# Re-ordering a fused attention and gated-MLP kernel: weight loads on one queue, a re-ordered prologue, earlier key features, PV in other slots

## The chip, the cores and the metric

The kernel runs on one core of one Trainium2 chip. The metric is the device time of one execution in microseconds (us). Five engines do the work: TensorE (PE) multiplies matrices, VectorE (DVE), ScalarE (ACT) and GpSimd (POOL) work on elements, and SyncE (SP) mostly issues DMA transfers. Within the fast state, the mean clock granted to PE still takes a few values, mainly 0.998 to 1.0, 0.993 and 0.987; this will matter.

## The reference, cut to what matters

```python
def reference(A_x, A_wq, A_wk, A_wv, A_wo, A_beta, B_x, B_w_gate, B_w_up, B_w_down, c, w_mod):
    # x: 2048 x 448; 16 heads of 28; 4 segments of 512 rows; MLP width 1792
    mod = (silu(c) @ w_mod)                       # six rows: sa, ca, ga, sb, cb, gb
    h = layernorm(x) * (1 + ca) + sa
    x = x + ga * attention(h, wq, wk, wv, wo, beta)
    h = layernorm(x) * (1 + cb) + sb
    x = x + gb * ((sigmoid(h @ w_gate) * (h @ w_up)) @ w_down)
    return x
# attention, per segment: causal softmax inside the segment (p @ v), plus a read of a
# memory M of all earlier segments: phi(q) @ M / (phi(q) @ z); then M += phi(k)^T v.
# The two are mixed with g = sigmoid(beta). phi(t) = t + 1 for t > 0, else exp(t).
```

## The kernel before: the parts that matter

The program is one hand-made order of instructions. Each engine executes its own share in that order. A queue `fill` holds jobs (projections, memory updates, output projection `wo`, MLP halves), and the loop over segments and head groups puts them between the three groups of logits of a unit. `later` delays cheap instructions in the order so that they don't block an engine.

```python
def mem_k(s, hc):                 # key features of the memory; 'pk' is their transpose, by DMA on SP
    ...
    phi(kT_of[s][:, hc, :], 3500, ("pk", s),
        lambda e: nc.sync.dma_start_transpose(pk[:, hc, :, :], e[:]))

def norm_t(self, i):              # layer norm of segments 2 and 3: transpose by DMA on SP
    self.norm(i)
    ...
    nc.sync.dma_start_transpose(self.h[:, :, i * P:(i + 1) * P], self.xn[:, i, :])   # 'hT'

def bias_rows():                  # sa @ wq, sa @ wk, sa @ wv, all in one PSUM buffer
    bp = m_f32("bp")
    for k in range(NK):
        for i, w in enumerate((wq_st, wk_st, wv_sb)):
            nc.tensor.matmul(bp[HP * i:HP * i + 1, 0:D], lhsT=sa_bf[...], rhs=w[...], ...)
    ...

def load_eng(w_sb):               # the up weights 'wu' are issued by ACT, all else by SP
    return nc.scalar if w_sb is wu_sb else nc.sync

early_loads = [load_wo, lambda: load_x(nc.sync, 3 * TPS, 4 * TPS), load_wm5] \
    + [piece_wd(f, min(f + 4, NFC)) for f in range(0, NFC, 4)] \
    + [piece(wg_sb, B_w_gate, k) for k in range(NK)] + [piece(wu_sb, B_w_up, k) for k in range(NK)]
fill.extend(sp(load_bw2))
fill.extend(spread(j0[3:6] + sp(late_consts) + j0[6:] + ln1_pe_jobs(1) + [ln1_start(2)] + m[0][0:1]
                   + j1[:4] + [ln1_start(3)] + j1[4:8], early_loads[:11], 1))
fill.extend(j1[8:] + [(1800, prep_b1)])
fill.extend(spread(j2[:2] + m[0][1:] + j2[2:3] + m[1][0:1] + j2[3:8], early_loads[11:], 2))
...
for s in range(NSEG):
    for hc in range(NHC):
        prev = (s, hc - 1) if hc else (s - 1, NHC - 1)
        for g in range(3):
            logits(s, hc, g)
            if fill and fill[0][1] is gate_up2:       # the up half of a gate-up pair
                fill.popleft()[1](); ...
            if prev[0] > 0 and g == 0:
                mem_read(*prev)
            if prev[0] >= 0 and g == 1:
                pv(*prev)
            ...
            debt = run_fill(pace[0] + debt)
            if prev[0] >= 0 and g == 2:
                otr(*prev)                            # DMA transpose 'oT' of the attention output
last = NSEG - 1
dj = down_jobs(last - 1)
mem_read(last, NHC - 1)
run_fill(2000)
pv(last, NHC - 1)
...
```

The softmax here doesn't subtract the row's maximum and nothing guards it: scores larger than these inputs give would overflow.

## Time and profile before

| | before |
|---|---|
| time, median of 3 runs | 262.42 us (261.68 to 262.72) |
| time of the profiled run | 263.58 us, clock 0.993 |
| span of the trace | 261.9 us |

The page's first part gives each engine's busy time; the clock row (PEclk) gives the granted clock in tenths, in 40 slices of the span. The prediction below shows both and reads the waits from them. The profiled run was 1.2 us slower than the median.

Two views of the kernel before: the first is SP's order of time (start, duration, line, output and input, number of instructions). The columns are the same in all orders of time below.

```profile
33.23 3.61 SPq L376 DMA_TRANSPOSE pk<-e  x2
36.93 5.31 SPq L283 DMA_TRANSPOSE hT<-xn  x4
42.33 1.22 SPq L376 DMA_TRANSPOSE pk<-e  x1
43.60 1.26 SPq L486 DMA_TRANSPOSE oT<-ou  x1
44.95 1.22 SPq L376 DMA_TRANSPOSE pk<-e  x1
```

The four hT transposes of segment 2 are issued in 5.31 us. The last pk goes out at 44.95. The second view is PE's order of time behind them; a bracket holds the idle time before a row and what ended it.

```profile
42.62 0.29 PE L414 MATMUL lg<-qT,kT 28*128 28x256 bf16 x4
43.62 1.02 PE L339 MATMUL pq<-hT,wq_sb 128*128 128x512 bf16 x4 [0.71 <-DMA hT<-xn]
...
49.24 0.38 PE L387 MATMUL dM<-vt,pk 128*128 128x116 bf16 x4 [2.27 <-DMA pk<-e]
```

PE begins segment 2 at 43.62 us and the last quarter of the first memory update at 49.24 us.

### The profile page before, as it was taken

Reading aid. Unit: us, or ns where it says so; the run is one execution under the profiler, and the core shown is the slowest. Engines: PE = TensorE matmul, PEld = TensorE weight load, DVE = VectorE, ACT = ScalarE, POOL = GpSimd, SP = SyncE. Lnnn points to the kernel's source line nnn. Section 1 sums busy time; section 2 is a strip of 40 time slices with the busy share of each in tenths; the row PEclk is TensorE's granted clock in tenths of the full one; section 3 lists DMA queues with packets and bytes.
Section 4 is the critical chain, followed back from the end, with each engine's and each line's share of the span. In section 5 each row is a group of like instructions: output and inputs, shape, how many; then the busy total and the mean of one; then the engine's idle time right before and its main releaser. Section 6 shows DMA issues by size and latency. Waiting matters only on the chain.

```text
span 261.9 us, 5307 instructions
## 1 busy us (share of the span) xinstructions
PE 243.3 (93%) x2066; PEld 113.3 (43%) x2066; DVE 175.6 (67%) x410; ACT 140.5 (54%) x175; POOL 78.5 (30%) x146
## 2 busy tenths in 40 slices
PE   7799997688988899899999999999998999999994
PEld 2434443333543343454544343445343445433352
DVE  5779899382898668878966576895754676544411
ACT  1368887549868597874617758534572210133300
POOL 3399255221346213243522121453030014000000
PEclk9999999997999999999999999999999999999999
DMA  5999934899912302210231010104200003200011
GB/s 147 276 249 255 327 75 101 146 178 194 97 28 54 29 16 46 57 23 20 46 91 40 20 22 0 24 20 95 58 15 9 20 0 67 86 0 0 3 35 35
DMA packets 40992, 19.66 MB, mean 75 GB/s; under 512 B 29704, under 2 KB 40072, under 8 KB 40968
## 3 DMA queue, kind: packets, MB, share of 16 engines
q1 hardware_dynamic: 39032, 16.92, 30.4%
q10 hardware_dynamic: 1936, 2.41, 4.2%
q8 instruction: 16, 0.26, 0.4%
q14 instruction: 8, 0.07, 0.1%
HBM read 10.67 MB, written 1.84 MB: 48 GB/s over the span
## 4 chain that ended last, share of the span: by engine, by line
PE 70%; DVE 10%; DMA 9%; ACT 5%; issue 3%; POOL 1%; ACTq 0%; SPq 0%; DVEq 0%
PE dps L546 16%; PE gps L520 13%; PE ups L537 12%; PE pq L339 5%; PE gps L525 5%; PE pwo L495 5%; PE acc L439 5%; PE lg L414 4%; DMA hT<-xn 3%; ACT pT L417 3%; DMA wm<-in_w_mod_dram 2%; PE pv L351 2%; DMA wv_sb<-in_A_wv_dram 2%; DVE st L265 2%; DVE xn L273 2%
## 5 line engine op out<-in xcount | busy, mean ns | idle before, releaser
L417 ACT ACTIVATE pT<-lg 128x2048 bf16<-128x2048 f32 (+1 forms) x48 | 76.8, 1599 | 26.8 <-PE lg L414 26.8
L528 ACT ACTIVATE tt<-gps 128x512 f32<-128x512 f32 x56 | 30.4, 595 | 57.5 <-PE gps L525 57.5
L425 POOL TENSOR_SCALAR_AFFINE_SELECT pT<-pT 128x512 bf16<-128x512 bf16 x64 | 41.5, 664 | 63.9 <-ACT pT L417 63.9
L540 DVE SCALAR_TENSOR_TENSOR fT<-tt,ups 128x512 bf16<-128x512 f32 x56 | 36.9, 685 | 31.4 <-PE ups L537 29.2
L546 PE MATMUL dps<-wd_sb,fT 128*128 128x448 bf16 x224 | 43.9, 352 | 0.0
L520 PE MATMUL gps<-hT,wg_sb 128*128 128x512 bf16 x168 | 41.2, 379 | 1.0 <-DVE t L451 1.0
L537 PE MATMUL ups<-hT,wu_sb 128*128 128x512 bf16 x168 | 41.1, 381 | 0.0
L546 PEld LDWEIGHTS <-fT 128*128 128x128 bf16 x224 | 21.5, 98 | 19.9 <-issue 0.2
L269 POOL TENSOR_SCALAR rs<-mv 128x1 f32<-128x1 f32 (+2 forms) x21 | 5.9, 282 | 61.2 <-DVE mv L266 58.4
L520 PEld LDWEIGHTS <-wg_sb 128*128 128x128 bf16 x168 | 15.8, 98 | 19.1 <-DVE t L451 1.6
L537 PEld LDWEIGHTS <-wu_sb 128*128 128x128 bf16 x168 | 14.2, 97 | 20.7 <-issue 6.6
L265 DVE BATCH_NORM_STATS2 st<-x_sb 128x6 f32<-128x448 bf16 x32 | 19.8, 619 | 2.5 <-DMA x_sb<-in_A_x_dram 2.0
L414 PE MATMUL lg<-qT,kT 28*128 28x512 bf16 (+3 forms) x256 | 17.3, 302 | 4.0 <-ACT pT L417 3.9
L439 PE MATMUL acc<-vt,pT 128*128 128x29 bf16 x640 | 18.7, 175 | 1.5 <-DVE t L470 1.0
L439 PEld LDWEIGHTS <-pT 128*128 128x128 bf16 x640 | 17.6, 96 | 5.2 <-issue 2.6
L273 DVE TENSOR_SCALAR xn<-x_sb,mv,rs 128x448 bf16<-128x448 bf16 x32 | 15.9, 512 | 4.6 <-POOL rs L270 4.6
L339 PE MATMUL pq<-hT,wq_sb 128*128 128x512 bf16 x64 | 17.8, 395 | 0.7 <-DMA hT<-xn 0.7
L550 DVE TENSOR_TENSOR ot<-dps,x_sb 128x448 bf16<-128x448 f32 x16 | 9.9, 621 | 12.2 <-PE dps L546 9.5
L525 PE MATMUL ups<-hT,wgu_sb 64*128 64x512 bf16 x56 | 17.5, 382 | 0.5 <-DVE t L451 0.5
L339 PE MATMUL pq<-hT,wk_sb 128*128 128x512 bf16 x64 | 16.5, 379 | 1.3 <-DVE t L451 1.1
L525 PE MATMUL gps<-hT,wgu_sb 64*128 64x512 bf16 x56 | 16.9, 381 | 0.0
L414 PEld LDWEIGHTS <-kT 28*128 28x128 bf16 x256 | 5.6, 91 | 22.1 <-issue 21.1
(100 smaller groups left out, 271.5 us busy)
## 6 DMA issues: line engine op xcount, KB each, us to landing
wm<-in_w_mod_dram SPq DMA_DIRECT2D x5, 392.0 KB, 9.2
out_dram<-ot SPq DMA_DIRECT2D x16, 112.0 KB, 1.7
x_sb<-in_A_x_dram SPq DMA_DIRECT2D x3, 448.0 KB, 4.8
wd_sb<-in_B_w_down_dram SPq DMA_DIRECT2D x3, 448.0 KB, 9.9
wg_sb<-in_B_w_gate_dram SPq DMA_DIRECT2D x3, 448.0 KB, 9.1
wu_sb<-in_B_w_up_dram ACTq DMA_DIRECT2D x3, 448.0 KB, 5.9
wm<-in_w_mod_dram ACTq DMA_DIRECT2D x1, 392.0 KB
wo_sb<-in_A_wo_dram SPq DMA_DIRECT2D x4, 98.0 KB
```

The lines of the kernel that those rows point to most:

```text
L265: nc.vector.bn_stats(st[:], self.srcs[i])
L339: nc.tensor.matmul(pq[:, 0:L], lhsT=head_cols(w_sb, k, hc), rhs=h[:, k, :], start=(k == 0), stop=(k == NK - 1))
L414: nc.tensor.matmul(lg[:, hs, wid:wid + nq], lhsT=kT[r, hc, kb * P:(kb + 1) * P], rhs=qT[r, hc, kb * P:L], start=True, stop=True, tile_posi ...
L417: nc.scalar.activation(pT[:, :, w0:w0 + wid], lg[:, :, 0:wid], AF.Exp, scale=scale)
L425: nc.gpsimd.affine_select(out=blk, in_=blk, compare_op=ALU.is_ge, fill=0.0, base=0, pattern=[[0, 4], [1, P]], channel_multiplier=-1)
L439: nc.tensor.matmul(accv[:, qb, hs, 0:ME], lhsT=pT[:, hs, c0:c0 + P], rhs=vt[:, kb, hc * 4 + hs, 0:ME], start=(kb == 0), stop=(kb == qb))
L520: nc.tensor.matmul(g[:, 0:L], lhsT=wg_sb[:, k, f], rhs=h[:, k, :], start=(k == 0), stop=False)
L525: nc.tensor.matmul(dst[:, 0:L], lhsT=wgu_sb[r:r + LW, f], rhs=h[r:r + LW, 3, :], start=first, stop=not first, tile_position=(r, 0))
L528: nc.scalar.activation(tt[:], g[:, 0:L], AF.Tanh, scale=0.5)
L537: nc.tensor.matmul(u[:, 0:L], lhsT=wu_sb[:, k, f], rhs=h[:, k, :], start=False, stop=(k == 2))
L540: nc.vector.scalar_tensor_tensor(ft[:], tt[:], 1.0, u[:, 0:L], op0=ALU.add, op1=ALU.mult)
L546: nc.tensor.matmul(dp[:, 0:D], lhsT=fT_of[(s, fc)][:, t * P:(t + 1) * P], rhs=wd_sb[:, fc, :], start=(fc == 0), stop=(fc == NFC - 1))
```

## The change

The intent is to take the last DMA issues off ACT, where one of them blocked an eviction and an exp, and to put them on SP right behind the other weights; to let the first projections start before the value weights are there; to issue the first key features' transposes earlier; and to run PV in a place where PE waited. The diff, cut to its core:

```diff
-    NWARM, EARLY, KEEP = (20, 2), 2400.0, (0, 2, 2, 4)
+    NWARM, EARLY, KEEP = 18, 2400.0, (0, 2, 2, 4)
...
-    def bias_rows():
-        bp = m_f32("bp")
+    def bias_rows(ws):
+        bp = warm[:, 4 - len(ws), :]
...
-    mod_cols(((0, 0), (1, 1)), False)
-    warm_up(NWARM[1])
+    mod_cols(((0, 0),), warm[:, 1, :])
+    for t in range(TPS):
+        ln0.norm(t)
+    mod_evac(((0, 0),))
...  # transposes of segment 0, then the second modulation, then q's bias alone:
+    evac_q, = bias_rows((wq_st,))
...
+    j0[0][1]()                                   # first q projection
+    evac_k, evac_v = bias_rows((wk_st, wv_sb))   # the biases that need wv
...
-    def load_eng(w_sb):
-        return nc.scalar if w_sb is wu_sb else nc.sync
...
-    fill.extend(spread(j0[3:6] + sp(late_consts) + j0[6:] + ln1_pe_jobs(1) + [ln1_start(2)] + m[0][0:1]
-                       + j1[:4] + [ln1_start(3)] + j1[4:8], early_loads[:11], 1))
+    fill.extend(spread(j0[3:6] + sp(late_consts) + j0[6:11] + m[0][0:1] + j0[11:] + ln1_pe_jobs(1) + [ln1_start(2)]
+                       + j1[:4] + [ln1_start(3)] + j1[4:8], early_loads, 1))
-    fill.extend(spread(j2[:2] + m[0][1:] + j2[2:3] + m[1][0:1] + j2[3:8], early_loads[11:], 2))
+    fill.extend(j2[:2] + m[0][1:] + j2[2:3] + m[1][0:1] + j2[3:8])
...
-                if prev[0] >= 0 and g == 1:
+                if prev[0] >= 0 and (g == 1 or g == 0 and s > 1 and pace[0] + debt <= 0) and prev in todo:
+                    todo.remove(prev)
                     pv(*prev)
...
+    if fill and fill[0][1] is gate_up2:
+        fill.popleft()[1]()
     mem_read(last, NHC - 1)
```

So there are five parts: the **prologue**, the **loads** on SP, the earlier **key job** (`m[0][0:1]`), the **PV** slots, and the **tail** (the up half ahead of the last memory read).

More of the change, by code (lines that the diff above doesn't have):

```diff
@@ L210, with mod_cols @@
     cp_of = {}
-    def mod_cols(jobs, evac=True):
-        cp = cp_of[0] = m_f32("cp")
+    def mod_cols(jobs, cp=None):
+        evac = cp is None
+        cp = cp_of[0] = m_f32("cp") if evac else cp
         for j, vi in jobs:
@@ L624, in pad_copy, with evac @@
             eng.tensor_scalar(dst, src, by, None, op0=ALU.mult)
-    def bias_rows():
-        bp = m_f32("bp")
+    def bias_rows(ws):
+        bp = warm[:, 4 - len(ws), :]
         for k in range(NK):
             r = P if k < 3 else LW
-            for i, w in enumerate((wq_st, wk_st, wv_sb)):
+            for i, w in enumerate(ws):
                 nc.tensor.matmul(bp[HP * i:HP * i + 1, 0:D], lhsT=sa_bf[0:r, k:k + 1], rhs=w[0:r, k, :],
                                  start=(k == 0), stop=(k == NK - 1), tile_position=(0, HP * i))
-        heads = lambda i: bp[HP * i:HP * i + 1, 0:D].rearrange("p (h d) -> p h d", d=Dh)
-        return [lambda: nc.scalar.copy(wq_sb[LW:LW + 1, 3, :, 0:Dh], heads(0)),
-                lambda: nc.vector.tensor_copy(wk_sb[LW:LW + 1, 3, :, 0:Dh], heads(1)),
-                lambda: nc.scalar.copy(wv_sb[LW:LW + 1, 3, :], bp[2 * HP:2 * HP + 1, 0:D])]
-    warm_up(NWARM[0])
+        def evac(i):
+            return lambda copy, dst: copy(dst, bp[HP * i:HP * i + 1, 0:D].rearrange("p (h d) -> p h d", d=Dh))
+        return [evac(i) for i in range(len(ws))]
+    warm_up(NWARM)
     ln0 = LN([x_sb[:, t, :] for t in range(TPS)], ("1", 0))
@@ L644 @@
     silu_ops()
-    mod_cols(((0, 0), (1, 1)), False)
-    warm_up(NWARM[1])
+    mod_cols(((0, 0),), warm[:, 1, :])
+    for t in range(TPS):
+        ln0.norm(t)
+    mod_evac(((0, 0),))
     pts = [m_bf16("lntr") for _ in range(NK)]
     for t in range(TPS):
-        ln0.norm(t)
-        if t == 1:
-            mod_evac(((0, 0), (1, 1)))
         for kc in range(NK):
             nc.tensor.transpose(pts[kc][:, t * P:(t + 1) * P], ln0.xn[:, t, kc * P:(kc + 1) * P], ident[:])
-    for k in range(2):
-        pad_copy(nc.scalar, wq_sb, wq_st, k)
-        pad_copy(nc.vector, wq_sb, wq_st, 2 + k)
+    mod_cols(((1, 1),), warm[:, 2, :])
     for kc in range(NK):
         ln0.pe_evac(pts[kc], kc, True)
-    evac_q, evac_k, evac_v = bias_rows()
-    evac_q()
+    mod_evac(((1, 1),))
+    evac_q, = bias_rows((wq_st,))
+    for k in range(NK):
+        pad_copy(nc.vector, wq_sb, wq_st, k)
+    evac_q(nc.scalar.copy, wq_sb[LW:LW + 1, 3, :, 0:Dh])
     for k in range(NK):
         pad_copy(nc.vector, wk_sb, wk_st, k)
-    evac_k()
-    evac_v()
+    tick(0)
+    j0, j1, j2, j3 = [proj_jobs(s) for s in range(NSEG)]
+    j0[0][1]()
+    evac_k, evac_v = bias_rows((wk_st, wv_sb))
+    evac_k(nc.vector.tensor_copy, wk_sb[LW:LW + 1, 3, :, 0:Dh])
+    evac_v(nc.scalar.copy, wv_sb[LW:LW + 1, 3, :].rearrange("p (h d) -> p h d", d=Dh))
     for k in range(NK):
@@ L671 @@
     ln1_start(1, True)[1]()
-    tick(0)
-    j0, j1, j2, j3 = [proj_jobs(s) for s in range(NSEG)]
-    for c, fn in j0[:3]:
+    for c, fn in j0[1:3]:
         fn()
@@ L694, in piece @@
             r = slice(0, LW) if w_sb is wg_sb else slice(LW, P)
-            return lambda: load_eng(w_sb).dma_start(wgu_sb[r, :], w[3 * P:D, :])
-        return lambda: load_eng(w_sb).dma_start(w_sb[:, k, :], w[k * P:(k + 1) * P, :])
+            return lambda: nc.sync.dma_start(wgu_sb[r, :], w[3 * P:D, :])
+        return lambda: nc.sync.dma_start(w_sb[:, k, :], w[k * P:(k + 1) * P, :])
     def piece_wd(f0, f1):
@@ L725 @@
     debt = 0.0
+    todo = {(s, hc) for s in range(NSEG) for hc in range(NHC)}
     for s in range(NSEG):
```

## The prediction

> **What bounds the kernel now.** I read the page first, then the waits of TensorE (PE), then the PE order of time in 5 us stretches, then the chain of work that ended last around the worst gaps, and the SyncE (SP) and ScalarE (ACT) queues beside them.
>
> ```profile
> PE 243.3 (93%) x2066; PEld 113.3 (43%) x2066; DVE 175.6 (67%) x410; ACT 140.5 (54%) x175; POOL 78.5 (30%) x146
> PEclk9999999997999999999999999999999999999999
> ```
>
> PE is busy 243.3 of 261.9 us, so 18.6 us of gaps are the whole stock that a reordering can draw on; no matmul of any weight is removed. The clock row has one dip, in the tenth slice (58.9 to 65.5 us). The waits say which gaps they are (engine, line, what it waited for; total, times, longest):
>
> ```profile
> PE lg L414 <- ACT pT L417: 3.9, 5, 1.8
> PE dM L387 <- DMA pk<-e: 2.3, 1, 2.3
> ...
> PE cp L224 <- DMA wm<-in_w_mod_dram: 1.0, 1, 1.0
> PE pq L339 <- DMA hT<-xn: 0.7, 1, 0.7
> ...
> PE mem L463 <- ACT tt L528: 0.5, 1, 0.5
> PE acc L439 <- ACT tt L528: 0.5, 1, 0.5
> ```
>
> The 3.9 us are one wait of 1.82 us (60.09 us), two of 0.78 us (106.51 and 150.71 us) and two of 0.25 us. The longest is explained by the ACT order of time and by the chain:
>
> ```profile
> 55.88 0.63 ACT L361 ACTIVATE e<-kT 128x512 bf16<-128x512 bf16 x1
> 58.00 0.49 ACTq L695 DMA_DIRECT2D wgu_sb<-in_B_w_up_dram  x1
> 58.53 0.58 ACT L342 CAST qT<-pq 128x512 bf16<-128x512 f32 x1 [2.01 <-PE pv L351]
> 59.01 1.03 ACT L417 ACTIVATE pT<-lg 128x1024 bf16<-128x1024 f32 x1
> ```
> ```profile
> 51.34 6.64 DMA hT<-xn
> 57.98 0.02 issue
> 58.00 0.49 ACTq L695
> ```
>
> ACT finishes an exp at 56.5 us and then stands in front of a weight-load issue until 58.0: the instruction order shows that each DMA waits for the DMA eight before it, and this one's lane belonged to the last hT transpose, which landed at 57.98. The label "<-PE pv" is misleading. Behind the issue stand the qT eviction and the exp that frees the logits buffer; PE gets it at 60.09 us. Straight after that gap the clock is low:
>
> ```profile
> 60.42 2.55 PE L351 MATMUL pv<-wv_sb,hT 128*128 128x448 bf16 x8
> 62.76 1.90 PE L339 MATMUL pq<-hT,wq_sb 128*128 128x512 bf16 x4
> ```
>
> The same groups take 1.68 (at 81.49) and 1.03 us elsewhere: 0.87 + 0.87 = 1.74 us lost, with 0.66 of the clock granted in 60 to 65 us.
>
> **What the Trainium skill says.** (1) "DMA: Bandwidth & Descriptors", Issuing engines are not separate DMA queues: loads issued by different engines share the same 16 DMA engines; issuing from several saves only sequencer time. The trace agrees and shows the price: the ACT issue cost 0.49 us plus 1.5 us of blocking. (2) "TensorE: Matmul & The Clock Gate", What's actually happening: the gate follows activity in a free-running window of about 3.4 us. The trace agrees in kind (the dip lasts about 4 us and follows the gap), but 2.27 us of idle at 47 us caused no dip, so I can't call it certain. (3) The same page, Architectural detail: ACT and DVE are strict FIFO. The blocked qT eviction above agrees. (4) "Perfetto Trace Analysis", DMA Instruction — HWDGE: the profiled length of an issue is descriptor generation, not data movement. The trace: each DMA transpose holds SP 1.22 us, and two loads of wd held it 1.90 and 2.66 us.
>
> **The change part by part.**
>
> *Loads.* All four wu/wgu issues (1.6 MB: three of 448 KB and one of 224 KB) go from ACT, 49.2 to 58.5 us, to SP right behind the wg loads, which SP finished issuing at 26.2 us; SP then idles until 33.2. ACT loses four issues and their waits. The 1.82 us gap goes: without the issue, qT and exp run 56.5 to 58.05 us, and PE came free at 58.27. **-1.8**. If PE then has no gap there, the dip has no cause: -1.74, which I take at three in four: **-1.3**.
>
> *Earlier key features.* The first memory-feature job moves ahead of the last value projection and four transposes. In the order, SP's pk transposes become three before the four hT transposes of segment 2 and one after, instead of two, four, one, then oT, then one. Before, the last pk was issued at 44.95 us behind an oT that waited for its input, and took 4.2 us to land; PE waited for it 2.27 us until 49.24. Now it follows hT directly, at about 42 to 43 us, and lands by 46 (transposes land in 2.3 to 3.6 us). The wait goes: **-2.3**.
>
> *Prologue.* Before, the first logits run at 16.52 and their exp at 16.97. The chain is: wv landing (12.54), 12 bias matmuls to 13.67, q eviction (ACT, 13.70, 0.52), k eviction (DVE, 14.25, 0.62), then statistics in front of the kT copy (15.77). The readers of the one bias buffer go one after another. After, q has its own buffer and needs neither wv nor the second modulation, so q projects at about 11.3 to 12.4 us. k and v still need wv: 12.54 + 1.0 = 13.55, k eviction to 14.17, last k matmul, kT copy first in line at about 14.45, logits at 15.2: 1.2 to 1.3 us earlier; the exp, behind the second qT copy, at about 15.9, 1.1 earlier. The two padding copies taken from ACT add 2 x 0.28 us to DVE, beside its old wait. But this gain must pass 43.62 us, where PE waits for hT of segment 2. The lane of the first pk is now the first wg load, which landed at 33.1 us (24.0 + 9.1): seven transposes at 1.22 us give 41.7 for hT complete in issue, 43.1 landed with 1.4 us after the last issue as before. The extra pk in front eats what the prologue gave. I count **-0.5** of 1.1.
>
> *PV in vacant slots.* The order shows just two moves of PV, one in each of segments 2 and 3: ahead of the wide second logits instead of behind. These are the places of the two 0.78 us waits; PV takes 1.1 us, so it covers them. The masks it needs come from the unit before. 1.56 at most, **-1.3** counted. In the tail the up half goes ahead of the memory read (1.3 us of matmuls over a 0.47 us wait). PV there again stands right behind a gate group, so its 0.47 stays: **-0.4**. Two warm-up matmuls more or less (22 to 18) lie beside DMA waits: 0.
>
> Sum: -1.8 - 1.3 - 2.3 - 0.5 - 1.3 - 0.4 = -7.6. After 70 us the rest is PE work, 192 us of it nearly without gaps, so these gains last to the end. I take 0.4 off for waits that come closer once PE is quicker (DVE is 4 to 4.9 of each 5 us busy in 15 to 45 us, and 4.8 in 70 to 75): 262.4 - 7.2 = **255.2 us**.
>
> **Rivals.** *A: SP and the rings become the bound at 33 to 45 us.* wu's 1.6 MB at the 366 GB/s seen for wg in 25 to 30 us is 4.4 us more in the queue: the old end of the burst, 33.5 us, becomes about 38. Transposes issued from 33.1 queue behind it, and SP may be held in issue as it was by wd (2.66 us). If the first pk issue ends at 36.5 instead of 34.3, hT lands at about 45.3, PE loses 1.7 us against before and the dip may come there instead: gain 7.2 - 2.2 - 1.3 = 3.7, time 258.7. For it: the seven transposes are back to back in any case. Against it: wu ends before hT is needed, and the rings drain faster than SP fills them with transposes. *B: everything hides.* The prologue gain would be eaten and the pk and ACT gaps replaced by hT and DVE waits: left are the PV and tail parts (1.7) and about half of the pk and ACT gaps (2.0), about 3.7, again 258.7. Against it: the two gaps have distinct causes, both removed. *C: all parts work,* with the dip gone and hT of segment 2 earlier by the whole prologue gain: -1.8 - 1.7 - 2.3 - 1.1 - 1.6 - 0.9 = -9.4, 253.0.
>
> **Range and chances.** The 2% mark lies at 257.2 us, that is at a gain of 5.2. The three gaps (PV, pk, ACT) alone give 5.4, so faster needs them plus anything else, or the dip. I hold that at 0.78; within 2% 0.20, mostly rival A; slower 0.02, as no work was added. The range, 252.5 to 258.8, runs from C to A.
>
> **What would show it.** The chain should hold no ACT issue; PE's waits should lack dM <- pk and the 1.8 us entry, the two 0.78 entries and one of the 0.47 ones. First logits at about 15.2 us, first exp at 15.9. hT of segment 2 seen by PE at 42.5 to 44 us: if later than 44.5, rival A. PEclk without a 7 near 60 us: if a dip shows elsewhere, my three-in-four was too high. PE busy should fall by about 1.7 us with the dip and the gaps from 18.6 to about 13. The prediction is wrong if the weight traffic delays transposes, or if waits on DVE (t, kT) grow by what was saved.

## The result and the profile after

| | before | after |
|---|---|---|
| median | 262.57 us (4 runs, 261.68 to 262.88) | 259.23 us (4 runs, 257.82 to 259.82) |
| clock of the runs after, with their times | | 0.992 (259.34), 1.0 (257.82), 0.993 (259.11), 0.993 (259.82) |
| ratio | | 0.987, 95% interval 0.982 to 0.992 |
| span of the trace | 261.9 us | 257.6 us |

A ratio here is the mean time of one kernel's fast runs over the mean time of the other's fast runs of the same rounds, so it is not quite the ratio of the medians. The change is 1.3% faster, which is within 2%. The predicted 255.2 us was missed: 259.23 lies above the upper end of the range that was given, 258.8, and the gain of over 2%, held at 0.78, did not come.

The page of after, for the same two rows as the prediction shows of before:

```profile
PE 242.7 (94%) x2062; PEld 112.7 (44%) x2062; DVE 175.2 (68%) x412; ACT 139.0 (54%) x173; POOL 79.5 (31%) x146
...
PEclk9889999999999999999999999999999999999999
```

PE's gaps fell from 18.6 us to 257.6 - 242.7 = 14.9 us (predicted: about 13). PE's busy time fell by only 0.6 us, where 1.7 us had been expected from a dip that would vanish. The dip of the clock is not gone; it is now in the second and third slices. PE's waits (what it waited for; total, times, longest):

```profile
PE warm L225 <- DVE silu L187: 1.5, 1, 1.5
...
PE pq L340 <- DMA hT<-xn: 1.2, 1, 1.2
...
PE lg L415 <- ACT pT L418: 0.5, 2, 0.2
...
PE acc L440 <- ACT tt L529: 0.5, 1, 0.5
...
PE gps L521 <- DVE hT L288: 0.3, 1, 0.3
...
PE pwo L496 <- DMA oT<-ou: 0.3, 1, 0.3
```

The waits that the change aimed at are gone as predicted: dM on pk (2.3), lg on ACT (3.9 in all, now 0.5) and mem on ACT (0.5). New are the wait on silu (1.5) and two small ones in the tail; the wait on hT grew from 0.7 to 1.2. But waits alone hide what happened, because an engine that arrives late waits less. The start of segment 2 in PE's order of time shows it:

```profile
44.58 0.29 PE L415 MATMUL lg<-qT,kT 28*128 28x256 bf16 x4
46.09 1.02 PE L340 MATMUL pq<-hT,wq_sb 128*128 128x512 bf16 x4 [1.23 <-DMA hT<-xn]
47.60 1.02 PE L340 MATMUL pq<-hT,wk_sb 128*128 128x512 bf16 x4 [0.49 <-DVE ou L449]
48.56 0.39 PE L415 MATMUL lg<-qT,kT 28*128 28x512 bf16 x4
48.88 1.01 PE L388 MATMUL dM<-vt,pk 128*128 128x116 bf16 x16
```

Segment 2 begins 46.09 - 43.62 = 2.47 us **later** than before. So the easiest way to find where the time went is to follow the difference of the two traces at the same piece of work (after minus before, us):

| point of PE's order | after - before | what happened since the row above |
|---|---|---|
| first logits (17.52, before 16.52) | +1.00 | prologue, with the clock dip in it |
| fifth logits (30.43, before 28.46) | +1.97 | the layer norm of segment 1 is later: its transposes on PE take 1.83 us instead of 0.91 |
| segment 2 starts (46.09, before 43.62) | +2.47 | the wait for hT is 0.52 longer (1.23 instead of 0.71) |
| last quarter of the first dM done | +0.27 | the pk wait is gone: -2.20 |
| the logits that waited for ACT (58.29, before 60.09) | -1.80 | the ACT stall is gone: -2.07 |
| logits behind it (61.10, before 64.59) | -3.49 | before's dip is not here: -1.69 |
| after the first moved PV (103.48, before 107.86) | -4.38 | -0.88 against the row at 100.22 (-3.50) |
| after the second moved PV | -5.12 | -0.88 against the row before it (-4.24) |
| output projection of the last segment (206.13, before 211.54) | -5.41 | |
| end of the span | -4.3 | the tail gives back 1.1 |

The gain is made in the middle, as predicted, and given away at both ends. In this trace most of the late start of segment 2 is there long before hT is waited for; hT is late too, as the second question shows.

### The profile page after: what moved, and what is told of

Same layout as the page of the kernel before. It is cut to its first block, busy times and chain, and to the rows that moved or that the text cites. A ratio compares the mean times of both kernels' runs of the same rounds, so it can differ in the third digit from the quotient of the medians.

```text
span 257.6 us, 5302 instructions
## 1 busy us (share of the span) xinstructions
PE 242.7 (94%) x2062; PEld 112.7 (44%) x2062; DVE 175.2 (68%) x412; ACT 139.0 (54%) x173; POOL 79.5 (31%) x146
## 4 chain that ended last, share of the span: by engine, by line
PE 69%; DVE 16%; DMA 4%; ACT 3%; issue 3%; POOL 2%; SPq 1%; POOLq 0%; DVEq 0%; ACTq 0%
PE gps L521 13%; PE ups L538 13%; PE dps L547 12%; PE pq L340 8%; PE acc L440 5%; PE gps L526 5%; PE lg L415 4%; PE pwo L496 4%; DVE st L266 4%; DVE xn L274 3%; DMA hT<-xn 2%; ACT pT L418 2%; DMA x_sb<-in_A_x_dram 2%; PE pv L352 1%; ACT tt L529 1%
## 5 line engine op out<-in xcount | busy, mean ns | idle before, releaser
L426 POOL TENSOR_SCALAR_AFFINE_SELECT pT<-pT 128x512 bf16<-128x512 bf16 x64 | 42.9, 688 | 58.8 <-ACT pT L418 58.8
L274 DVE TENSOR_SCALAR xn<-x_sb,mv,rs 128x448 bf16<-128x448 bf16 x32 | 14.1, 458 | 5.7 <-POOL rs L271 5.7
L271 POOL TENSOR_TENSOR rs<-rs,mhalf 128x1 f32<-128x1 f32 (+2 forms) x21 | 13.8, 658 | 1.8
```

The source lines that it names most:

```text
L426: nc.gpsimd.affine_select(out=blk, in_=blk, compare_op=ALU.is_ge, fill=0.0, base=0, pattern=[[0, 4], [1, P]], channel_multiplier=-1)
```

## The experiments

Fourteen kernels were run, all correct. The kernel before ran in the same rounds each time, with medians of 262.05 to 262.51 us. "Dip-free" counts the runs whose mean clock is 0.998 or more; of the kernel before these are 14 of 42.

| run | what | median us | ratio, 95% interval | dip-free |
|---|---|---|---|---|
| after | all five parts | 259.23 | 0.987, 0.982 to 0.992 | 1 of 4 |
| e1 | after without the prologue | 260.13 | 0.991, 0.988 to 0.994 | 0 of 6 |
| e2 | prologue alone | 263.64 | 1.0045, 1.002 to 1.008 | 0 of 6 |
| e3 | after without the tail | 258.73 | 0.985, 0.981 to 0.988 | 3 of 6 |
| b1 | loads, key job, PV | 258.90 | 0.986, 0.983 to 0.990 | 2 of 6 |
| e4 | loads alone | 260.90 | 0.992, 0.988 to 0.997 | 3 of 6 |
| e5 | key job alone | 260.73 | 0.992, 0.988 to 0.997 | 3 of 6 |
| e8 | after, wu loads at 53 us | 259.73 | 0.988, 0.984 to 0.992 | 4 of 6 |
| b2 | b1, wu loads at 53 us | 259.18 | 0.988, 0.984 to 0.992 | 2 of 6 |
| e6 | PV alone | 260.76 | 0.994, 0.992 to 0.996 | 2 of 6 |
| e7 | tail alone | 262.65 | 1.0025, 0.999 to 1.006 | 0 of 6 |
| e9 | after with 24 warm-ups | 258.47 | 0.985, 0.982 to 0.988 | 3 of 6 |
| b3 | b1, wu loads behind an oT, at 65 us | 256.50 | 0.979, 0.977 to 0.982 | 4 of 6 |
| e10 | after, wu loads behind that oT | 257.37 | 0.984, 0.981 to 0.987 | 5 of 6 |
| e11 | e9 with the hT gap filled | 258.07 | 0.985, 0.983 to 0.987 | 5 of 5 |

### First question: the prologue, and is the tail worth it?

The theory was that the new prologue costs time through the dip it starts, and the rival that the wu transfers delay hT whatever the prologue does.

**e1** puts before's prologue back into after. **e2** puts after's prologue alone into before.

```diff
# e1, against after
-    NWARM, EARLY, KEEP = 18, 2400.0, (0, 2, 2, 4)
+    NWARM, EARLY, KEEP = (20, 2), 2400.0, (0, 2, 2, 4)
     # and mod_cols, bias_rows and the prologue's body as they were before
# e2, against before: the same lines the other way round
```

> The changed kernel with the prologue of the kernel before (order of modulation, bias rows, 20 + 2 warm-ups, first key copies), all other parts kept. Theory P (the new prologue costs about 2.5 to 3 us at the point where segment 2's features arrive): first logits at 16.5 us as before instead of 17.5, PE sees hT of segment 2 at about 43.5 instead of 46.1, and the time is 2 to 3 us under the changed kernel, 256.5 to 257.5. Rival R (the weight loads in the SP queue and the pk transposes ahead of hT are what delays hT): hT of segment 2 still arrives at 45.5 or later, the time stays within 0.7 us of 259.2.

> The kernel before with only the new prologue. Theory P: first logits at about 17.5 us, PE two microseconds late at 37 us, hT of segment 2 at 45.5 to 46.5, and as the later waits (pk, the ACT weight-load issue) may swallow part of it, the time is 1 to 3 us over before: 263.5 to 265.5. Rival R: the prologue is neutral or better: hT at 43.6 or earlier, 261.5 to 262.8.

Measured: e1 260.13 us and e2 263.64 us. e2 came out as theory P had it: first logits at 17.57 us, segment 2 at 45.67 us although wu is still loaded late and by ACT. The prologue alone makes the kernel slower, by 0.45% with an interval that excludes 1. But without it the rest is not quicker than after: e1's time fits neither theory, it is 0.9 us over after. In e1 the first logits are at 16.64 us, 0.88 earlier than in after, and yet segment 2 begins at 46.02 us, as in after (46.09), now behind a wait of 3.0 us. What the prologue wins or loses is swallowed by the wait for hT. The rival was right for the place at 46 us in e1, and theory P in e2: each of the two causes is enough for a start of segment 2 near 46 us.

**e3** takes the tail's up half back out of after. **b1** takes the three parts that looked good (loads, key job, PV) without prologue and tail.

```diff
# e3, against after
     dj = down_jobs(last - 1)
-    if fill and fill[0][1] is gate_up2:
-        fill.popleft()[1]()
     mem_read(last, NHC - 1)
# b1, against before: loads, key job and PV of the change; prologue and tail as before
```

> The changed kernel without the up half moved ahead of the last memory read. Theory T (the move delays the last PV by a whole gate-up group, so that the last output projection and the last layer norm come into the open): two waits of 0.47 us come back near 194 to 200 us, but the pwo wait on oT (0.30) and the gate wait on hT (0.34) go; the end is 0.6 to 1.0 us earlier, about 258.4. Rival: those waits come from PE arriving earlier, not from the move; then they stay, and the time is 0.3 us worse, 259.5.

> Loads on SP, early key job and PV slots, with the prologue and the tail of the kernel before. If theories P and T both hold and add up: 2.5 + 0.8 us under the changed kernel, 255.5 to 256.5. If the prologue's loss is hidden by hT anyway (rival R): 258.4 or more.

Measured: e3 258.73 us and b1 258.90 us, both somewhat under after with intervals that overlap its own. Runs of a like clock show no difference: without a dip 257.88 and 257.85, and 257.82 in the one such run of after. In e3's profile the prologue has no dip, and the first logits are at 15.97 us, 0.55 earlier than before; segment 2 still begins only at 45.83, and in b1 at 45.68. All four kernels with the early wu loads so far start segment 2 between 45.7 and 46.1 us.

### Second question: which part makes hT late?

**e4** is the loads alone and **e5** the key job alone. In e4 the SP queue has wu's issues but only two pk ahead of hT; in e5 there are three pk but no wu.

```diff
# e4, against before
-        return lambda: load_eng(w_sb).dma_start(w_sb[:, k, :], w[k * P:(k + 1) * P, :])
+        return lambda: nc.sync.dma_start(w_sb[:, k, :], w[k * P:(k + 1) * P, :])
-                       + j1[:4] + [ln1_start(3)] + j1[4:8], early_loads[:11], 1))
+                       + j1[:4] + [ln1_start(3)] + j1[4:8], early_loads, 1))
# e5, against before
-    ... + j0[6:] + ln1_pe_jobs(1) + [ln1_start(2)] + m[0][0:1]
+    ... + j0[6:11] + m[0][0:1] + j0[11:] + ln1_pe_jobs(1) + [ln1_start(2)]
```

> The kernel before with only the up-weight loads moved to the SP queue behind the gate loads. Theory Q (their 1.6 MB keep the queue full until about 38 us and hold SP in the issue of the transposes behind them): one transpose issue takes over 2.5 us instead of 1.2, hT of segment 2 reaches PE at 44.4 to 45.0 instead of 43.6, the pk wait of 2.3 us stays, the 1.8 us wait near 60 us goes: 1 us gained, 261 to 261.8. Rival K (it is the third pk transpose ahead of hT that delays it): hT at 43.6, 1.8 us or more gained, 260.5.

> The kernel before with only the first memory-feature job moved forward, so three pk transposes precede hT and the fourth follows at once. Theory Q: without the up weights in the queue the transposes start at about 31 us and hT is not delayed (PE at 43.4 to 44.0), the 2.3 us wait on pk goes: 2 us gained, 260.0 to 260.8. Rival K: hT at 44.8 or later, the gain under 1.2 us.

Measured: 260.90 and 260.73 us. The times are alike, the traces are not. PE's start of segment 2 in e4, then in e5:

```profile
46.15 1.39 PE L339 MATMUL pq<-hT,wq_sb 128*128 128x512 bf16 x4 [3.04 <-DMA hT<-xn]
47.33 1.91 PE L339 MATMUL pq<-hT,wk_sb 128*128 128x512 bf16 x4
```
```profile
44.20 1.02 PE L339 MATMUL pq<-hT,wq_sb 128*128 128x512 bf16 x4 [1.42 <-DMA hT<-xn]
```

The loads alone move the start by 46.15 - 43.62 = 2.53 us, the key job alone by 0.58 us. SP's order of time in e4 says how; compare it with before's above:

```profile
27.35 3.02 SPq L693 DMA_DIRECT2D wu_sb<-in_B_w_up_dram  x3
30.70 0.47 SPq L692 DMA_DIRECT2D wgu_sb<-in_B_w_up_dram  x1
33.43 3.88 SPq L376 DMA_TRANSPOSE pk<-e  x2
37.40 7.42 SPq L283 DMA_TRANSPOSE hT<-xn  x4
```

The wu issues end at 31.2 us, and hT's first issue begins at 37.40, only 0.47 later than before. But the four issues then take 7.42 us instead of 5.31. At that moment the DMA engines still move weights, most likely wu: of the packets from 36 to 48 us, 280 have 2 to 8 KB, and before has none of these. This is the throughput row (GB/s) of the stretch from 36 to 48 us, in slices of 0.3 us, in e4:

```profile
GB/s 347 346 346 418 387 400 283 146 140 201 161 166 137 85 90 47 12 24 24 20 86 290 237 275 261 259 253 103 10 86 200 153 2 29 279 129 0 0 148 257
```

For some 2 us from 36 on, the engines run at 346 to 418 GB/s, where before has bursts of at most 275 with pauses. I read this as a queue in which the transposes stand, with their issue on SP held up behind it; the trace shows only that the two coincide. In b1 the single record is the clearest, the first hT transpose (before: 1.22 us):

```profile
37.67 2.77 SPq L283 DMA_TRANSPOSE hT<-xn  x1
```

In e5 the same issue begins at 37.55 us, takes 1.22 us, and segment 2 begins 1.48 us earlier than in b1. What follows: in e4 and b1 most of the extra time before segment 2 comes with the early loads, and 0.58 us (e5) with the additional pk. The expectation for e4, 44.4 to 45.0 us, was still too early.

After's own profiled run looks different, so that trace alone would not have shown this:

```profile
32.72 6.83 SPq L377 DMA_TRANSPOSE pk<-e  x3
39.64 5.16 SPq L284 DMA_TRANSPOSE hT<-xn  x4
```

No hT issue is stretched here (1.22 to 1.23 us each). They begin late, because the three pk begin 1.57 us later than in e10 (31.15 us), where the prologue has no dip. In both runs the three pk take 6.8 us and not 3 x 1.22 = 3.7, as each is issued when VectorE has finished its key features: the last operation on them ends at 32.69, 35.91 and 38.32 us in after, and the issues begin at 32.72, 35.94 and 38.35.

The same two experiments also bear on two parts of the prediction. In e5 the pk wait is gone. In e4 the ACT stall of 1.82 us is gone (longest lg wait on ACT 0.8), but this alone proves little, as e6 and e7 below will show; b1's trace, without a dip and without the stall, shows it better. The second slow line of e4's PE view, a projection of 1.91 instead of 1.02 us, is the clock dip, which now follows the hT gap.

**e8** and **b2** test it the other way: the wu loads stay on SP but are issued at about 53 us, past all of these transposes.

```diff
# e8, against after (b2: the same edit on b1)
-        + [...wg...] + [piece(wu_sb, B_w_up, k) for k in range(NK)]
+        + [...wg...]
         wm[3] = load_wm(nc.sync, 3)                 # in prep_b1
+        for k in range(NK):
+            piece(wu_sb, B_w_up, k)()
```

> The changed kernel, but the four up-weight loads are issued by SP only behind the last modulation weights (at about 53 us). Theory Q: hT of segment 2 reaches PE at 44.0 to 45.0 instead of 46.1 (the new prologue's lateness of up to 2 us remains in it), its wait falls under 0.5 us unless the prologue is quick, no dip after it; 1 to 2 us under the changed kernel, 257.3 to 258.2, and the ACT stall stays away. Rival: the delay of hT comes from VectorE or the third pk, then it stays at 45.5 or later and the time at 259.

> Late loads on SP, early key job, PV slots, the prologue and tail of the kernel before. Theory Q: PE goes into segment 2 at about 43.6 us, no wait on pk, no ACT stall: 4.1 (pk and ACT) + 1.7 (PV) under before, 256 to 257 even without any help from the clock; best of all kernels. Rival: the late loads delay pk or oT of segment 1 and PE waits at 65 to 75 us instead; 258.5.

Measured: 259.73 and 259.18 us, so no gain over after and b1. Segment 2 now begins at 44.66 and 44.38, as the theory says, and four of e8's six runs are free of dips. But the same collision comes back at another place, this time with the oT transposes. PE's order of time in e8:

```profile
66.29 0.36 PE L496 MATMUL pwo<-wo_sb,oT 128*128 128x448 bf16 x1 [0.18 <-DMA oT<-ou]
67.95 1.88 PE L496 MATMUL pwo<-wo_sb,oT 128*128 128x448 bf16 x9 [1.29 <-DMA oT<-ou]
```

These waits are in neither before nor after. My expectation of a gain failed because I had looked for a place where no hT is waited for; the rival written down for b2 had named oT, a wait at 65 to 75 us and 258.5 us.

### Third question: a place where nothing is waited for; PV, the tail and the warm-ups alone

**b3** is b1 with the wu loads right behind the last oT transpose of segment 0 in the order. There the next transpose on SP comes some 4 us later.

```diff
# b3, against b1
                     otr(*prev)
+                    if (s, hc) == (1, 0):
+                        for k in range(NK):
+                            piece(wu_sb, B_w_up, k)()
     # and wu out of early_loads, as in e8
```

> As the best candidate with late loads, but the four up-weight loads are issued right behind the last oT transpose of segment 0 (SP about 65 us), where SP stands idle until about 71 us. Theory Q (a weight load delays exactly the transposes that are queued behind it): hT of segment 2 at 44.4 us, no wait of pwo on oT over 0.4 us, no ACT stall; the first up matmul at about 86 us finds its weights. Span 254 to 255.5 without a clock dip, time 255.7 to 257.5. Rival: the transposes of the second layer norm at 71 us are then late and the gates wait: time 259 again.

Measured: 256.50 us, ratio 0.979 (0.977 to 0.982): 2.1% under before, with an interval that lies on both sides of the 2% line, and about 1% under after. SP's order of time in b3:

```profile
63.63 1.19 SPq L486 DMA_TRANSPOSE oT<-ou  x1
64.87 1.53 SPq L693 DMA_DIRECT2D wu_sb<-in_B_w_up_dram  x3
66.86 0.49 SPq L692 DMA_DIRECT2D wgu_sb<-in_B_w_up_dram  x1
70.48 1.23 SPq L283 DMA_TRANSPOSE hT<-xn  x1
```

The transpose behind the loads takes its usual 1.23 us. Segment 2 begins at 44.93, and no pwo waits for oT. This is the version that beats both kernels; it did not run in the same rounds as after, whose ratio to before is 0.987 (0.982 to 0.992).

**e6** is PV alone and **e7** the tail alone.

```diff
# e6, against before: only
-                if prev[0] >= 0 and g == 1:
+                if prev[0] >= 0 and (g == 1 or g == 0 and s > 1 and pace[0] + debt <= 0) and prev in todo:
+                    todo.remove(prev)
# e7, against before: only
+    if fill and fill[0][1] is gate_up2:
+        fill.popleft()[1]()
     mem_read(last, NHC - 1)
```

> The kernel before with only PV moved into the slot ahead of the wide logits where the budget is spent. Expected: the two waits of 0.78 us on the exp go, nothing else changes: 1.5 us gained in the trace between 100 and 155 us, time 260.7 to 261.2. Rival (PV only trades one wait for another): within 0.4 us of before.

> The kernel before with only the up half moved ahead of the last memory read. Theory T: one 0.47 us wait goes, but pwo now waits for oT (0.3) and the last gates may wait for hT: 0.3 to 0.8 us slower from the last logits to the end, time 262.5 to 263.3. Rival (as I predicted): 0.4 us faster, 262.1.

Measured: e6 260.76 us, 0.6% faster; 262.45 - 260.76 = 1.7 us of the medians. PE's order of time around the first move, in before and then in after:

```profile
105.35 0.38 PE L463 MATMUL mem<-rm,e 128*128 128x116 bf16 x4
106.51 0.40 PE L414 MATMUL lg<-qT,kT 28*128 28x384 bf16 x8 [0.78 <-ACT pT L417]
106.84 1.17 PE L439 MATMUL acc<-vt,pT 128*128 128x29 bf16 x40
```
```profile
101.85 0.38 PE L464 MATMUL mem<-rm,e 128*128 128x116 bf16 x4
102.06 1.16 PE L440 MATMUL acc<-vt,pT 128*128 128x29 bf16 x40
103.15 0.40 PE L415 MATMUL lg<-qT,kT 28*128 28x384 bf16 x8
```

PV (`acc`, 1.17 us) now stands where PE waited 0.78 us for ACT to free the logits buffer. Nothing waits any more.

e7 took 262.65 us, ratio 1.0025 (0.999 to 1.006), which includes 1: in the time it is inconclusive. In the trace it is not. The part removes the 0.47 us wait of the last memory read, but it delays the last PV by one more gate-up step, so that its output is transposed later. The tail of after, where before has no wait at the output projection:

```profile
200.60 1.15 PE L440 MATMUL acc<-vt,pT 128*128 128x29 bf16 x40 [0.47 <-ACT tt L529]
...
206.13 0.73 PE L496 MATMUL pwo<-wo_sb,oT 128*128 128x448 bf16 x3
207.16 2.63 PE L496 MATMUL pwo<-wo_sb,oT 128*128 128x448 bf16 x13 [0.30 <-DMA oT<-ou]
```

e7 shows the same 0.30 us wait, at 210.54. From the last logits to the end of the span, the nine profiles without the tail part take 68.9 to 69.5 us, a mean of 69.1; the seven with it take 69.2 to 70.0 us, a mean of 69.6. So it costs about 0.5 us in the traces, with ranges that overlap (69.5 in e3 without it, 69.2 in e9 and e11 with it). The times do not settle it: among runs with one dip, e7 is 0.1 us over before, after 0.2 us under e3, and e1 1.0 us over b1 (two runs), which differ by the tail alone. No pair shows the gain that was predicted.

**e9** is after with 24 instead of 18 warm-up matmuls, to fill PE's 1.5 us gap before the first modulation.

```diff
-    NWARM, EARLY, KEEP = 18, 2400.0, (0, 2, 2, 4)
+    NWARM, EARLY, KEEP = 24, 2400.0, (0, 2, 2, 4)
```

> The changed kernel with 24 warm-up matmuls instead of 18, so PE has work until the modulation weights and silu are there (8.3 us). If the clock dips of the prologue come from the 1.5 us gap that the fewer warm-ups left, none of the runs has a low clock before 20 us, and more runs than one in four show a mean clock of 1.0. If the dip only moves to the hT wait at 46 us, the share of runs with a clock of 0.993 stays as it is and the time stays at 259.0 to 259.5.

Measured: 258.47 us, 0.8 us of the medians under after, in another set of runs and with overlapping intervals. PE's prologue in after, then in e9:

```profile
8.32 0.54 PE L225 MATMUL warm<-silu,wm 112*128 112x1 bf16 x16 [1.46 <-DVE silu L187]
...
11.11 1.74 PE L632 MATMUL warm<-wd_sb,sa_bf 128*1 128x448 bf16 x4 [0.37 <-DVE cols L237]
12.78 1.87 PE L340 MATMUL pq<-hT,wq_sb 128*128 128x512 bf16 x4
...
17.52 0.39 PE L415 MATMUL lg<-qT,kT 28*128 28x512 bf16 x4
```
```profile
8.39 0.54 PE L225 MATMUL warm<-silu,wm 112*128 112x1 bf16 x16
...
11.16 1.00 PE L632 MATMUL warm<-wd_sb,sa_bf 128*1 128x448 bf16 x4 [0.37 <-DVE cols L237]
...
16.03 0.40 PE L415 MATMUL lg<-qT,kT 28*128 28x512 bf16 x4
```

In after's profile a gap of 1.46 us is followed by half-rate matmuls (four bias matmuls in 1.74 instead of 1.00 us) and the first logits come at 17.52; without the gap they come at 16.03. The number of warm-ups does not fix this gap: the same 18 left 1.36 us in e2's profile, also with a dip, but 0.89, 0.60 and 0.41 us in those of e3, e8 and e10, without one. e9's dip is not gone either: it now lies behind the hT gap (2.32 us), in the eighth slice.

```profile
PEclk9999999799999999999999999999999999999999
```

### Last question: the place alone, and the dips alone

By now 12 kernels were run and the cause of the miss was still open in one respect: how much is the late hT itself, and how much are the dips that follow such gaps? **e10** changes in after only the place of the wu loads. **e11** leaves the loads early, and fills both gaps with useless matmuls whose result is overwritten (24 warm-ups, and ten copies of one projection matmul at the hT wait), so that PE is not idle while hT is late.

```diff
# e10, against after: wu out of early_loads; behind otr(*prev) as in b3
# e11, against after: NWARM = 24, and in proj_qk
         pq = m_f32("pq")
+        if s == 2 and hc == 0 and w_sb is wq_sb:
+            for _ in range(10):
+                nc.tensor.matmul(pq[:, 0:L], lhsT=head_cols(w_sb, 0, hc), rhs=hT_of[("1", 1)][:, 0, :], start=True, stop=True)
         for k in range(NK):
```

> The changed kernel with one difference: the four up-weight loads are issued behind the last oT transpose of segment 0 instead of behind the gate loads. Theory Q (the loads' place in the SP queue is what took the gain): hT of segment 2 reaches PE at 44.4 to 45.0 instead of 45.8 to 46.1, no new wait at pwo; 1.0 to 1.5 us under the changed kernel in runs of the same clock, median 257.2 to 258.2. Rival: the new prologue holds the same gain back (VectorE late), then hT at 45.5 or later and 258.7 to 259.3.

> The changed kernel with 24 warm-up matmuls and ten further throw-away matmuls (2.2 us) where PE waits for hT of segment 2; they write the buffer that the real ones overwrite, so the result is right. Theory D (the dip follows the gap of PE): with both gaps filled nearly all runs have a mean clock of 0.998 or more, and the time is that of the dip-free runs, 257.3 to 258.3, though PE does more work. Rival: the dips come at random or from power, then half of the runs or more still show 0.993 and the time is 258.5 to 259.5.

Measured: e10 257.37 us, with five of six runs without a dip; segment 2 begins at 44.66, behind a wait of 1.37 us that is put down to an ACT exp. e11 258.07 us (five runs were timed), and none of the five has a dip. The clock row of e11, which is the same in e10:

```profile
PEclk9999999999999999999999999999999999999999
```

So with both gaps filled no dip came in five runs, although the real projection of segment 2 still begins only at 45.62 us; after and e9 had dips in six of their ten runs. This speaks for the gaps as the cause, with few runs. The 16 profiles agree and show that length matters: of ten PE gaps of 1.8 us or more (the start of the program left out) eight were followed by a dip, of twelve gaps of 1.1 to 1.8 us two, both at 8 us (after and e2), and none of the gaps of 0.8 to 1.1 us that each kernel has between 73 and 90 us. One dip, b3's in the old prologue, followed two gaps of 0.97 and 0.85 us. With the loads early, the hT gap of the traces in which PE is in time is 2.3 to 3.0 us; with them late on SP (e8, b2, b3, e10) it is 1.3 to 1.4 us.

This also allows to ask what a dip costs, by comparing the runs of one kernel with and without it:

| kernel | mean without a dip (runs) | mean with one dip (runs) | difference |
|---|---|---|---|
| before | 262.04 (14) | 262.45 (26) | 0.4 |
| e6 | 260.75 (2) | 260.73 (4) | 0.0 |
| e5 | 260.95 (3) | 260.63 (3) | -0.3 |
| e8 | 259.83 (4) | 259.34 (2) | -0.5 |
| b2 | 259.06 (2) | 259.09 (2) | 0.0 |
| e4 | 259.84 (3) | 261.43 (2) | 1.6 |
| e3 | 257.88 (3) | 259.58 (3) | 1.7 |
| e9 | 257.80 (3) | 259.08 (3) | 1.3 |
| b3 | 256.46 (4) | 257.66 (2) | 1.2 |
| b1 | 257.85 (2) | 259.17 (2) | 1.3 |
| after | 257.82 (1) | 259.42 (3) | 1.6 |
| e10 | 257.33 (5) | 259.09 (1) | 1.8 |

The numbers of runs are small. In before, e5, e6, e8 and b2 a dip costs 0.4 us or nothing that can be seen; in the other seven it costs 1.2 to 1.8 us. The traces of e6 and e7 give a reason. Their dip lies at 47 to 55 us (granted clock 0.76 to 0.82), and they still load wu by ACT; yet the logits that waited 1.82 us for ACT in before, at 60.09 us, wait for nothing. In e7:

```profile
49.12 0.57 PE L387 MATMUL dM<-vt,pk 128*128 128x116 bf16 x4 [2.33 <-DMA pk<-e]
59.71 0.40 PE L414 MATMUL lg<-qT,kT 28*128 28x512 bf16 x4
```

Before had no dip up to there and was no earlier: the slow PE used up the time in which it would have stood for ACT. So a dip costs little where a later wait would have ended at the same time anyway. It fits that the kernels in which it is cheap have such a wait in their traces (before and e5 on ACT near 60 us, e8 and b2 on oT near 68 us; e6 has before's order of loads), and that the other seven have none of 1 us or more between 50 and 70 us. No run tests this by itself.

So e10's gain over after, 1.9 us of the medians, has two parts. Dip-free runs compare as 257.33 (five runs of e10) with 257.82 (the one of after) or 257.80 (e9): 0.5 us is the earlier hT itself. The other 1.4 us are dips that no longer come. Dip-free traces agree: e10 starts segment 2 0.96 us before e11, but its second projection then waits 0.34 us for VectorE (`ou`), and from the next logits (46.98 and 47.44 us) to the last ones (186.17 and 186.64 us) the lead stays near 0.5 us. The same comparison of b3 with b1 (256.46 with 257.85, two runs) has 1.4 us. These sets ran in different rounds, whose dip-free runs of before differ by up to 0.5 us, so I give it as about 0.5 us, at most 1.4.

## Why the prediction was wrong, point by point

**Loads off ACT (-1.8 predicted): right for the trace, not for the usual run.** The stall of 1.82 us is gone in every kernel whose wu loads are on SP, and the difference of the traces moves by -2.07 there. But in e6 and e7, with the loads still on ACT, a dip at 47 to 55 us had removed it too. So -1.8 and the -1.3 of the dip do not add up in a run of that kind; before's profiled run, with its dip behind the stall, paid both.

**Earlier key features (-2.3): right.** The pk wait is gone in after and in e5; the difference moves by -2.20. On its own (e5, 0.992) the part is worth less than that, because the additional pk ahead of hT delays segment 2 by 0.58 us.

**The failed step: "this gain must pass 43.62 us ... I count -0.5 of 1.1."** I let seven transposes go out back to back at 1.22 us each from 33.1 us and so had hT issued at 41.7 and landed at 43.1. Neither half held. The three pk are not back to back: they take 6.8 us, paced by VectorE, so hT's last issue ended at 42.8 us in e5 and 43.2 us in e10 even with no early loads. And the issues do not keep their length while wu's 1.6 MB is under way: 2.77 us for the first of hT in b1, 7.42 us for the four in e4. (Already in before one hT issue, at 46.33 us, took 2.30 us, against "each DMA transpose holds SP 1.22 us".) In after's profiled run the dip of the prologue made the pk late instead. hT came so that segment 2 began at 45.6 to 46.1 us in every kernel with the early loads, and at 44.2 to 44.9 with the third pk ahead but without them. In place of -0.5 the traces show +2.1 (b1) to +2.5. This is rival A in kind: it put hT at about 45.3 us and the time at 258.7, though the issue that it saw held up was the first pk (1.3 us in b1) and not hT. I argued against it with "wu ends before hT is needed", although the working beside it had the burst ending at about 38 us, past hT's first issue at 36.9. The rival's own number should have overruled the argument.

**The second failed step: the dip, "which I take at three in four: -1.3".** It failed twice. First, the dip is tied to PE gaps, not to the one gap that the change removes: in after's trace it sits behind the silu gap; in e1, e3, e4 and e9 behind the hT gap; in e6 and e7 at the pk gap; in b3 in the old prologue; e2 has one in the prologue and one at the pk gap. Three of after's four runs have one. Second, I read its price, 1.7 us, from one trace, in which the dip lay at 60 us over dense work, and this was a run 1.2 us above the median. In the usual run of before a dip costs 0.4 us. So before had almost nothing to lose, and after pays about 1.5 us in most of its runs: in place of -1.3 the runs show about +1.1. The Trainium skill, "TensorE: Matmul & The Clock Gate", section What's actually happening, has a window of 3413 ns and, for this gate, two rates only. The steps of the mean clock agree: a mean of 0.993 over 258 us is 0.007 x 258 = 1.8 us of lost clock, by estimate one stretch of about 3.6 us at half rate. It also calls the window free-running, which fits that runs of one and the same kernel differ in whether they have a dip; no run here shows the window's phase.

**Prologue (counted with the step above), and warm-ups "0".** The mechanism of the earlier start works when no dip comes: 15.97 us for the first logits in e3 against a predicted 15.2 and 16.52 before, so 0.55 us of the predicted 1.2. It is lost again by the fifth logits, also without a dip: e10 has 28.87 us there, 0.41 later than before's 28.46. The fewer warm-ups (four fewer, 22 to 18, not two) were not free: in after's trace the gap of 1.46 us behind them is followed by a dip that makes the first logits 1.0 us later than before. Alone, the prologue costs 0.45% (e2).

**PV (-1.3): right, and a little too low.** Both waits went, 0.88 us each in the traces; e6 has 1.7 us (by its interval 1.0 to 2.2).

**Tail (-0.4): wrong, and in the traces wrong in sign.** The memory wait went, but the last PV, its transpose and the output projection became later; by the traces it costs about 0.5 us, by the times a cost is not shown.

Put together against the medians: the late hT with the prologue made about 2.6 us of the miss (-0.5 predicted, +2.06 in b1's trace, which has no dip), the dip 2.4 and the tail 0.9. PV was 0.5, the ACT stall and the pk wait together 0.2 better than predicted, and the 0.4 held back for waits that come closer was not needed. That is 2.6 + 2.4 + 0.9 - 0.5 - 0.2 - 0.4 = 4.8 us, against 259.23 - 255.2 = 4.0 us.

**What stays open.** The sum is 0.8 us too large, and its likeliest term is the late hT: of 0.96 us of lateness at 45.6 us only about 0.5 arrives at the end (e11 against e10), as the earlier kernel then waits for VectorE. It also takes terms from one trace and from medians together, so it is a rough balance. Why e1 is slower than after, although it lacks the prologue that is slow alone, is open: all six runs of e1 have a dip, but they are also 0.8 us over the three runs of after that have one (260.19 and 259.42). And the new prologue loses its start on DVE: there a coefficient operation on 16 columns waits 1.11 us for ACT and then takes 1.61 us, where it took 0.30 before, and the normalization of segment 1 stands behind it (its transposes start at 26.44 instead of 25.39 us). The dip-free e10 has the same wait and the same 1.61 us; why the operation takes longer is not shown.

## What to carry to other kernels

Before a bulk load is moved to an emptier queue, ask which small, urgent transfers follow it there within the time that its bytes need, not within the time that its issues need, and when their inputs are ready; the right place here was behind the last urgent transpose (b3, 256.50 us, against 259.23 for the same loads early). Count with a clock dip behind a gap of PE of about 2 us or more (8 of 10 here); do not credit its disappearance while another gap of that size is left, read its price from runs with and without it, not from one trace, and don't add it to a wait behind it that would have hidden it. When parts are judged by one profile, compare the start of the same piece of work in both traces, because a wait that shrinks can belong to an engine that only came later.

## What the Trainium skill lacked or had wrong

- "TensorE: Matmul & The Clock Gate", section Why this matters for your kernels, advises "No PE-idle gaps >~3µs between matmul bursts". Here dips follow shorter gaps: 1.46 us in after, 1.82 us in before, 2.32 us in e9; and with gaps of up to 1.37 us left, five of six runs (e10) had none. In before's trace the pk gap of 2.27 us was not followed by a dip, in e6 and e7 the like gap (1.98 and 2.33 us) was, so the length alone does not decide it. Over the 16 profiles, 8 of 10 gaps of 1.8 us or more and 2 of 12 of 1.1 to 1.8 us were followed by a dip.
- "Perfetto Trace Analysis", section DMA Instruction — HWDGE, has the profiled length of an issue as lock wait, descriptor generation and semaphore push, and does not say that it can grow while earlier transfers are still moving. Here the issue of the same transpose took 1.22 us in e5 and 2.77 us in b1 behind 1.6 MB of loads, with the next issue on SP only after it; 2.30 us also occurs behind transposes alone (before, at 46.33 us).
- "DMA: Bandwidth & Descriptors", section Issuing engines are not separate DMA queues, says that issuing from several engines only saves time of the sequencer that starts them. For the bandwidth no run here contradicts it, but it lacks the advice that follows for order: the same four loads on the same engine cost 259.23 us when issued at 26 to 30 us and 257.37 us when issued at about 65 us (after and e10), of which about 0.5 us is the transposes behind them and the rest clock dips.
